# First two batches transposed from fp32 and loaded a second time, a new order of the weight loads, and paired squares, in a fused attention and feed-forward kernel

## The chip, the cores and the metric

The kernel runs on one core of one Trainium2 chip. The metric is device microseconds of that core, the median over the executions of a call; below, "before" in a comparison always means executions of the kernel before in the same call, on the same chip. The span of a profile is some 1.8 us shorter than the time of the same execution.

## The reference

Two small attentions between `x` (8 batches, 8 heads, 512 tokens, 64 wide) and `state` (32 rows per head), then a feed-forward layer with squared ReLU over all 4608 resulting rows. Cut to what matters:

```python
scores = scale * x @ state.T          # x reads the state
a      = softmax(scores);   xread = a @ state
scores2 = scale * state @ x.T         # the state reads x
a2     = softmax(scores2);  sread = a2 @ x          # needs x itself
x = concat([xread, sread], axis=2) -> (4608, 512)
h = x @ w_in                          # 512 x 2048
g = s * relu(h)**2 + b
out = g @ w_out                       # 2048 x 512
```

## The kernel before

A small scheduler written in the kernel takes a list of operations with estimated durations, needs, buffers and order constants, and fixes the order of instructions on each engine. PE (TensorE) forms `M = state @ w_in` for each batch and then `h = a.T @ M`; ScalarE (ACT) does the exponentials, logarithms and most ReLUs; VectorE (DVE) squares, makes pair sums and scales the output. The heavy output products start with `o <- wo,g`.

The parts that the change touches. The weights and the x of batches 2 and up are loaded by one software queue issued from GpSimd (POOL), in a fixed order; the x of batches 0 and 1 comes in fp32 by other queues, is cast to fp16 (`xn`), and transposed by PE:

```python
SEQ = "wi0 wi2 wo1 wi1 wo0 wi3 wo2 wo3 x2 x3"      # wi: w_in chunk, wo: w_out part
...
add(AC(0.5) if n < 3 else (DV(0.35), AC(0.5)), ..., cast_x(b, i),       # 8 casts fp32 -> fp16
    [("xf", b, i)], [("x", b, i)], [("u", f"xf{n // 2}"), ("xn", f"x{b}")])
...
def xT_mm(b, i):                                   # 8 transposes, fp16
    ps = A[b][f"xTps{i}"] = att_ps([P, 4, 2, P], FP16, ...)
    mm(ps[:, hh, k, :], xn[b][:, head_of(i, hh), ...], ident16, is_transpose=True)
```

`V` is the product `a2 @ x`, named "slot reads" in the title of the change. It needs `xn`, and `aT`: the exponentials `E`, transposed by a DMA that SyncE (SP) issues, four such DMAs for the first two batches:

```python
def aT_dma(b, g):
    nc.sync.dma_start_transpose(a["aT"][:, g], a["E"][g])
...
add(PEt(0.22), kV, V_mm(b), [("aT", b, 0), ("aT", b, 1)], [("V", b)],
    [V_b, ("aT", f"aT{b}"), xn_b], tiled=True)
...
def square(name, f):                               # one block of 512
    ENG[e].tensor_mul(g_of(name, f), g_of(name, f), g_of(name, f))
```

Near 33 us PE also forms the "bias sums" (`wsum_ps`), which need all four parts of `w_out`.

The softmax here doesn't subtract the row's maximum and nothing guards it: scores larger than these inputs give would overflow.

## Time and profile before

| | kernel before |
|---|---|
| time, median of 3 (range) | 210.81 us (210.65 to 210.86) |
| span of the profiled execution (211.43 us, 0.6 above the median) | 209.6 us |
| PE / DVE / ACT busy | 97% / 84% / 65% |
| first `h` matmul / first output matmul | 15.24 / 24.07 us |
| the four `aT` transpositions landed | 36.0 to 38.7 us |

Its busy line, its chain of work, the windows of the start and the timeline rows there are in the prediction. Needed for comparison is the page: the row of the software queue (packets, MB, share of the 16 DMA engines' span), what was read from memory, and the group of the squares (busy us, mean ns, idle before).

```profile
q0 software_dynamic: 12896, 14.68, 37.4%
...
HBM read 17.33 MB, written 8.91 MB: 125 GB/s over the span
...
L813 DVE TENSOR_TENSOR g<-g 128x512 f16<-128x512 f16 x128 | 52.7, 423 | 5.1 <-ACT g L807 3.3
```

```profile
40.00:45.00 5.00, 5.00 (x98) 2.22 (x96) 4.96 (x9) 1.67 (x3) 3.73 (x6) 1.00 0.67 183
```

### The profile page before, as it was taken

What the parts mean: (1) busy time and instruction counts of PE and PEld (TensorE: products, weight loads), DVE (VectorE), ACT (ScalarE), POOL (GpSimd) and SP (SyncE); (2) the same over time, 40 slices, a digit from 0 to 9 for tenths busy, and PEclk for the clock granted to TensorE, in tenths of its full rate; (3) what the DMA queues carried; (4) which work ended last, traced back from release to release, by engine and by line L of the source; (5) the groups of instructions that cost most, each with busy time, mean ns of one, the idle gap of its engine ahead of it and who ended that gap; (6) DMA issues with size and microseconds to landing.
All of it is one profiled execution on the core that took longest, in us unless ns stands there. A gap on an engine that the chain in (4) does not pass through costs nothing.

```text
span 209.6 us, 4981 instructions
## 1 busy us (share of the span) xinstructions
PE 202.7 (97%) x1962; PEld 131.3 (63%) x1962; DVE 176.0 (84%) x406; ACT 135.7 (65%) x302; POOL 41.1 (20%) x65
## 2 busy tenths in 40 slices
PE   7998999999999999999999999999999999999993
PEld 2532344434865766677667766776667777788882
DVE  2569999998779898899989998998899989867762
ACT  3899899658578857775776658675767545236300
POOL 0850000150250225022501331121012001200000
PEclk9999999999999999999999999999999999999999
DMA  6999999589898763933298339421302111310132
GB/s 194 299 191 204 214 205 159 124 183 119 193 159 116 119 141 77 160 103 112 69 122 160 105 70 157 107 81 49 100 9 100 50 53 50 100 59 2 47 133 75
DMA packets 42344, 25.00 MB, mean 119 GB/s; under 512 B 26448, under 2 KB 40528, under 8 KB 42320
## 3 DMA queue, kind: packets, MB, share of 16 engines
q0 software_dynamic: 12896, 14.68, 37.4%
q1 hardware_dynamic: 29136, 9.84, 24.9%
q8 instruction: 15, 0.25, 0.5%
q10 hardware_dynamic: 288, 0.16, 0.4%
q14 instruction: 9, 0.07, 0.1%
HBM read 17.33 MB, written 8.91 MB: 125 GB/s over the span
## 4 chain that ended last, share of the span: by engine, by line
PE 87%; DMA 9%; POOL 2%; SPq 0%; DVE 0%; issue 0%
PE o L214 49%; PE h L214 24%; DMA wo<-in_moe_w_out_dram 7%; PE Mps L214 4%; PE h_sr L214 3%; PE osr L214 3%; DMA xf<-in_x_dram 2%; PE V L214 1%; PE D L214 1%; POOL wi L362 1%; PE T L214 1%; PE wsum_ps L214 0%; SPq L256 0%; POOL wo L372 0%; DVE c_sr L1052 0%; PE bias_ps L214 0%
## 5 line engine op out<-in xcount | busy, mean ns | idle before, releaser
L807 ACT ACTIVATE g<-h 128x512 f16<-128x512 f32 x125 | 72.8, 599 | 39.4 <-PE h L214 38.7
L214 PE MATMUL h<-a,M 128*128 128x512 f16 x256 | 74.0, 379 | 0.7 <-ACT g L807 0.7
L813 DVE TENSOR_TENSOR g<-g 128x512 f16<-128x512 f16 x128 | 52.7, 423 | 5.1 <-ACT g L807 3.3
L214 PEld LDWEIGHTS <-pd 128*128 128x128 f16 x448 | 42.6, 98 | 20.7 <-issue 4.2
L214 PEld LDWEIGHTS <-g 128*128 128x128 f16 x400 | 38.7, 98 | 20.1 <-issue 1.6
L214 PE MATMUL o<-u,pd 128*128 128x256 f16 x336 | 48.8, 273 | 0.0
L214 PE MATMUL o<-wo,g 128*128 128x256 f16 (+1 forms) x288 | 45.8, 296 | 0.3 <-DMA wo<-in_moe_w_out_dram 0.3
L1064 POOL DMA_DIRECT2D out_dram<-c x24 | 16.4, 682 | 100.8 <-DVE c L1052 97.4
L214 PEld LDWEIGHTS <-M 128*128 128x128 f16 x256 | 24.5, 98 | 12.8 <-issue 3.4
L306 ACT CAST M<-Mps 128x512 f16<-128x512 f32 x41 | 22.8, 592 | 4.7 <-PE Mps L214 4.7
L1052 DVE SCALAR_TENSOR_TENSOR c<-o,sb_cols,bias_bc 128x512 f32<-128x512 f32 x28 | 21.0, 750 | 5.6 <-PE o L214 5.1
L829 DVE TENSOR_TENSOR pd<-g 128x1024 f16<-128x1024 f16 x28 | 19.2, 687 | 0.4
L1052 DVE SCALAR_TENSOR_TENSOR c<-o,sb_cols,c 128x512 f32<-128x512 f32 x21 | 15.7, 750 | 4.5 <-PE o L214 4.1
L214 PE MATMUL o<-u,g 128*128 128x256 f16 x112 | 17.2, 273 | 0.0
L308 DVE CAST M<-Mps 128x512 f16<-128x512 f32 x23 | 15.1, 683 | 0.5 <-PE Mps L214 0.4
L214 PE MATMUL o<-wo,pd 128*128 128x256 f16 x112 | 15.4, 273 | 0.0
L385 POOL DMA_DIRECT2D xn<-in_x_dram x18 | 13.9, 824 | 0.0
L550 ACT ACTIVATE E<-T 128x256 f16<-128x256 f32 x32 | 11.4, 386 | 2.5 <-PE T L214 2.5
L840 DVE TENSOR_TENSOR pd<-g,pd 128x512 f16<-128x512 f16 x28 | 11.7, 419 | 0.3
L838 DVE TENSOR_TENSOR pd<-g,pd 128x512 f16<-128x512 f16 x28 | 11.7, 416 | 0.1
L573 ACT ACTIVATE D<-D 128x512 f32<-128x512 f32 x16 | 9.3, 588 | 1.9 <-PE D L214 1.9
L580 ACT ACTIVATE R<-D 128x512 f16<-128x512 f32 x16 | 9.4, 597 | 0.4
(80 smaller groups left out, 158.5 us busy)
## 6 DMA issues: line engine op xcount, KB each, us to landing
out_dram<-c POOLq DMA_DIRECT2D x24, 256.0 KB, 2.6
xf<-in_x_dram SPq DMA_DIRECT2D x8, 256.0 KB, 5.0
wi<-in_moe_w_in_dram POOLq DMA_DIRECT2D x4, 512.0 KB, 9.9
wo<-in_moe_w_out_dram POOLq DMA_DIRECT2D x4, 512.0 KB, 16.2
xn<-in_x_dram POOLq DMA_DIRECT2D x16, 128.0 KB, 4.2
xn<-in_x_dram POOLq DMA_DIRECT2D x2, 512.0 KB, 15.1
out_dram<-osb POOLq DMA_DIRECT2D x4, 256.0 KB, 2.9
out_dram<-c SPq DMA_DIRECT2D x4, 256.0 KB, 2.5
```

Of the source, the lines that this page charges most:

```text
L214: return nc.tensor.matmul(out, lhsT, rhs, start=start, stop=stop, tile_position=tp, is_transpose=is_transpose, skip_group_check=True,)
L306: nc.scalar.copy(dst, src)
L308: ENG[e].tensor_copy(dst, src)
L385: nc.gpsimd.dma_start(out=xn[b][:, h0:h1].rearrange("p h c d -> p h (c d)"), in_=x[b, h0:h1].rearrange("h (q c) d -> q h (c d)", q=P),)
L550: nc.scalar.activation(a["E"][g][:, 256 * m : 256 * m + 256], a["T"][m][:, g, :], AF.Exp, scale=scale, **kw)
L807: nc.scalar.activation(g_of(name, f), OSB["h", name, f], AF.Relu)
L813: ENG[e].tensor_mul(g_of(name, f), g_of(name, f), g_of(name, f))
L829: nc.vector.tensor_tensor(pd[:, :, 0:2], g4[:, :, 1:2, :].to_broadcast((P, 2, 2, t)), g4[:, :, 0:4:3, :], ALU.subtract,)
L838: nc.vector.tensor_tensor(pd[:, :, 2], g4[:, :, 3], pd[:, :, 0], ALU.subtract)
L840: nc.vector.tensor_tensor(pd[:, :, 3], g4[:, :, 2], pd[:, :, 2], ALU.subtract)
L1052: nc.vector.scalar_tensor_tensor(t, src, s_bc, add, ALU.mult, ALU.add)
L1064: ENG[e].dma_start(dst[:, rows:SCH:2, hD * h : hD * h + hD], SN[b, name])
```

## The change

The intent is to start PE's real work earlier. The cast of `x` leaves the head of the kernel: PE transposes the fp32 tiles directly. As `V` still needs `x` in fp16, the x of batches 0 and 1 is loaded a second time, casting on the way, behind the weights ("late for the slot reads"). Three chunks of `w_in` now come ahead of most of `w_out`. Squares go two blocks at a time, the logarithm of the softmax sums goes to SBUF (freeing a PSUM slot), and all order constants of the scheduler are retuned. The core of the diff:

```diff
-    for n in range(8):                       # the eight casts of x
-        add(AC(0.5) if n < 3 else (DV(0.35), AC(0.5)), ..., cast_x(b, i), ...)
+    add(DV(0.15), -31, lambda e: nc.vector.tensor_copy(ident32, ident16), ...)
...
-    SEQ = "wi0 wi2 wo1 wi1 wo0 wi3 wo2 wo3 x2 x3"
+    SEQ = "wi0 wi1 wi2 wo0 wo1 wi3 wo2 x2 wo3 x0 x1 x3"
...
-            ps = A[b][f"xTps{i}"] = att_ps([P, 4, 2, P], FP16, ...)
-                    mm(ps[:, hh, k, :], xn[b][...], ident16, is_transpose=True)
+            ps = A[b][f"xTps{p}"] = att_ps([P, 2, 2, P], FP32, ...)
+                    mm(ps[:, hh, k, :], xf_part(b, p)[:, hh, P * k : P * k + P], ident32, is_transpose=True)
...
-            nc.scalar.activation(A[b][f"D{g}"], A[b][f"D{g}"], AF.Ln)
+            A[b][f"L{g}"] = opool.tile([P, S], FP32, ..., tag="osb")
+            nc.scalar.activation(A[b][f"L{g}"], A[b][f"D{g}"], AF.Ln)
...
-            PEt(0.22), kV, V_mm(b), [("aT", b, 0), ("aT", b, 1)], [("V", b)],
+            PEt(0.22), kV, V_mm(b), [("aT", b, 0), ("aT", b, 1)] + ([("x", b, i) for i in range(4)] if b < 2 else []), [("V", b)],
...
-            ENG[e].tensor_mul(g_of(name, f), g_of(name, f), g_of(name, f))
+            g = G[name, f // 4][:, f % 4 : f % 4 + 2, :]
+            ENG[e].tensor_mul(g, g, g)
```

Cut: the retuned constants, the scheduler's small additions, other PSUM slots for the first scores and the warm-ups, and the bias that ACT may now do.

## The prediction

> **What bounds the kernel now.** I read the page first: its busy line and its chain of work that ended last.
>
> ```profile
> PE 202.7 (97%) x1962; PEld 131.3 (63%) x1962; DVE 176.0 (84%) x406; ACT 135.7 (65%) x302; POOL 41.1 (20%) x65
> ...
> PE 87%; DMA 9%; POOL 2%; SPq 0%; DVE 0%; issue 0%
> PE o L214 49%; PE h L214 24%; DMA wo<-in_moe_w_out_dram 7%; PE Mps L214 4%; PE h_sr L214 3%; PE osr L214 3%; DMA xf<-in_x_dram 2%; PE V L214 1%; PE D L214 1%; POOL wi L362 1%; PE T L214 1%; PE wsum_ps L214 0%; SPq L256 0%; POOL wo L372 0%; DVE c_sr L1052 0%; PE bias_ps L214 0%
> ```
>
> TensorE (PE) is the bound. The only part of the chain that is not PE is at the start: a load of x (2%), the issue of weight loads, and a wait for w_out (7%). The windows by stage say when. Columns: stretch, its length, then busy us of each engine.
>
> ```profile
> core 0: us, PE busy (x) PEld busy (x) DVE busy (x) ACT busy (x) POOL busy (x), PEclk, DMA share, GB/s
> 0.00:5.00 5.00, 3.81 (x9) 1.16 (x9) 1.14 (x10) 1.90 (x2) 0.20 (x4) 1.00 0.62 185
> 5.00:10.00 5.00, 4.52 (x52) 2.56 (x51) 2.60 (x8) 3.74 (x8) 3.75 (x6) 1.00 1.11 312
> 10.00:15.00 5.00, 4.51 (x55) 1.91 (x53) 3.11 (x7) 4.90 (x13) 3.52 (x5) 1.00 1.21 190
> 15.00:20.00 5.00, 4.30 (x31) 1.48 (x30) 4.57 (x11) 4.77 (x10) 0.24 (x1) 1.00 1.24 204
> 20.00:25.00 5.00, 4.52 (x33) 1.58 (x32) 4.63 (x12) 4.81 (x10) 0.00 (x0) 1.00 1.23 215
> 25.00:30.00 5.00, 5.00 (x38) 2.03 (x37) 4.95 (x16) 4.30 (x10) 0.28 (x1) 1.00 1.24 207
> ...
> 109.93:131.69 21.76, 21.76 (x229) 14.91 (x227) 19.93 (x44) 15.48 (x33) 5.59 (x8) 1.00 0.74 119
> ```
>
> From 25 us on PE is busy in every window; one batch takes 21.77 us and PE works all of it, with VectorE (DVE) at 92% beside it. Before 25 us PE is idle or runs warm-up matmuls, while ScalarE (ACT) is at 95 to 98% and the DMA engines are saturated. So whatever the change does for DVE or ACT after 25 us is worth nothing directly, and only what starts PE's real work earlier, or later makes it wait, moves the end. The timeline of the start shows the first matmul on h, the first output matmul, and what that one waited for; the POOL rows date the landings of the second, seventh and eighth weight.
>
> ```profile
> 13.22 0.41 PE L214 MATMUL Mps<-wi,stT 64*32 64x512 f16 x8
> ...
> 15.24 1.02 PE L214 MATMUL h<-a,M 128*128 128x512 f16 x4
> ...
> 18.58 0.24 POOL L429 CAST stf<-wo 128x2 f32<-128x2 f16 x1 [5.05 <-DMA wo<-in_moe_w_out_dram]
> ...
> 24.07 1.02 PE L214 MATMUL o<-wo,g 128*128 128x512 f16 x4 [0.35 <-DMA wo<-in_moe_w_out_dram]
> ...
> 29.08 0.28 POOL L415 CAST sb_in<-wo 128x2 f32<-128x2 f16 x1 [10.27 <-DMA wo<-in_moe_w_out_dram]
> ...
> 31.67 0.47 POOL L426 CAST stf<-wo 128x2 f32<-128x2 f16 x1 [2.31 <-DMA wo<-in_moe_w_out_dram]
> ```
>
> Landings, issue plus "to landing" in the views of the load lines: w_in chunk 0 at 12.2, the eight weights in queue order 12.2, 14.8, 18.5, 21.0, 24.0, 26.5, 29.0, 31.6, then x of batch 2 (issued 12.6, 22.5 to landing) at 35.1. One weight per 2.8 us, in queue order.
>
> **What the Trainium skill says.** "DMA: Bandwidth & Descriptors", section "SWDGE vs HWDGE vs iDMA": one software queue is allocated, and each DMA engine round-robins between that and the hardware queues. The trace agrees: landings come in issue order, and x of batch 2, beside the transposes issued from 30.8 on, took 3.5 us after its predecessor instead of 2.5. "VectorE: DVE Perf Modes", "Mode 2×_1P": two results per cycle for 16-bit data, one for fp32 or PSUM. Agrees: the fp16 square of 128x512 takes 423 ns and the fp16 subtraction of 128x1024 takes 687, while a 512-wide cast from fp32 PSUM takes 683. "ScalarE: Activation LUTs": ScalarE writes PSUM faster than SBUF. Hardly here: the logarithm that stays in PSUM takes 588 ns, the exponential that goes to SBUF 597. "TensorEngine Tiling (Array Packing)": switching the tiling mode drains PE. Agrees: four h matmuls take 0.86 us start to start, 0.96 where a tiled group follows.
>
> **The change part by part.** Durations are those of the page; but two relus in a row take 1.09 us of ACT and five squares 1.85 us of DVE in the timeline, so the pitch is 0.5 on ACT, and 0.36 (fp16) or 0.6 (from PSUM) on DVE.
>
> 1. *No cast of x.* Six ACT casts (3.7 us) and two DVE casts (0.9) go. The copies after the transposes become eight of 512 fp32 elements: two on ACT, six on DVE (6 x 0.69 = 4.1 us, against 3.2 for all copies before). Net about 3 us off ACT, 1.5 us onto DVE, all before 13 us. The chain to the first exponential loses a cast (0.62): transposes after the 9 warm-ups at 5.1, copy by 6.3, second by 7.1, scores at 7.6, first exponential at 8.0 (before: 8.71). Second pair: 8.75 against 9.78. ACT then has no xn cast between, so the last reciprocal of batch 0 ends at 11.8 rather than 13.18. fp32 transposes may cost PE two to four times the 55 ns of fp16; no trace shows it yet. PE has room: there were 24 warm-ups.
> 2. *But w_in chunk 0 lands at 12.2 in both.* The first product M then runs at 12.3 instead of 13.22, its casts end near 13.4 (DVE has the fourth copy of batch 1 just before), the scores of batch 1 come first in PE's order, and the first h starts at 14.2: 1.0 us earlier, not the 1.4 that ACT alone would give.
> 3. *Loads.* First landings stay 12.2 and 14.8; w_in chunk 2 comes third (near 17.5), w_out part 0 fourth, near 20.9 instead of 24.0. The program's order puts 8 h tiles ahead of the first output group (before: 12), so it is due when it lands. Walking ACT in steps of 0.5 from 15.1 (h0, two logarithms, R, h2, h3, R, h4, h5, an M cast, h6, h7) gives h7 on PE at 19.9 and one M group behind it at 20.5 to 20.8. First output group: 21.0.
> 4. *From there to the bias sums.* Nine groups of 0.86 and one M pair of 0.66 to the first group with w_out part 2, waiting 0.3 for w_in chunk 3 (26.5): 29.7. Then five groups, one transposition (0.22) and a mode switch (0.1): the bias sums are due at 34.4. By then PE has done two h tiles (0.86) and two output groups (1.73) more than before at its bias sums (32.82), so the equal point of the old kernel is 35.4. **Gain: 1.0 us.**
> 5. *What is loaded late.* x of batch 2 now stands ahead of w_out part 3, so the two exchange landings: part 3 comes at 34 to 35.1. The bias sums need it: 0 to 0.7 us of waiting, 0.2 expected. Then x of batches 0 and 1 (1 MB each, read from HBM) follow for V. At 2.6 to 3.5 us each beside the transposes, and up to 5.7 where transposes are dense (x of batch 3 took 7.7 from issue), the second lands at 41 to 46. V stands in PE's fixed order about 9.7 us behind the bias sums: 44.1 to 44.8. Expected wait 0.3.
> 6. *Pairs of squares.* 64 of about 0.69 for 128 of 0.423: 54 - 44 = 10 us less DVE. It takes DVE from 92 to about 88% of a batch, off the path.
> 7. *Logarithm to SBUF, bias on ACT.* Same durations; a PSUM slot comes free sooner. Nothing on the path.
> 8. *Steady state and end.* The built order has the same matmuls and the same 54 mode switches after the first h; the last group is the same. Zero, if no buffer or relu makes PE wait.
>
> Sum: -1.0 + 0.2 + 0.3 = -0.5 us. The table of order constants was retuned throughout, which my walk cannot value after 45 us; I allow 0.6 more for that and for a start that is better than walked. Predicted 210.81 - 1.1 = 209.7.
>
> **The rivals.** *A, the reload stalls PE.* V waits for the second x; if the queue gets only half of the engines (as x of batch 3 did), it lands at 47, PE waits 2 to 3 us, and the time is 211.5 to 213. For: saturated DMA up to 33 us and eight transposes behind. Against: the DMA share falls to 0.7 to 0.8 after 35. *B, the start gains in full.* DVE and ACT keep up, part 3 and x arrive in time, and the first output group at 21.0 carries nearly all: up to 2.5 us, 208.3. Against: ACT at 95% and four fewer h tiles done by then. *C, the steady state loosens.* New orders bunch h tiles; ACT needs 0.5 per relu plus casts, PE would wait a few tenths in each of six batches: 211 to 212. Against: ACT is at 70% per batch. *D, nothing.* Old loads bounded the start, new ones do: 210.8.
>
> **Range and chances.** What the start could give is limited: PE lacks about 2.3 us of work between its first h and 24 us, plus 1 to 1.4 ahead of that. So faster by over 2% (4.2 us) would need more than there is: 0.03. Slower by 2% needs rival A with over 4 us: 0.04. Range 208.2 (B) to 211.4 (mild A or C).
>
> **What the new profile would show.** Right: first h near 14.2, first output group at 20.8 to 21.3, waits of PE on wo and xn under 1 us together, batches still 21.8 us, DVE squares near 44 us. Wrong: PE waiting more than 1.5 us for xn or wo, the first output group after 22, a batch that differs from 21.77 by over 0.2, or PE idle after 50 us.

## More of the kernel before

```profile
DMA to landing us min/median/max: 2.5/3.9/5.2
```

PE has no gap there, the DMA engines are two thirds busy, and the slowest of the four `aT` lands 5.2 us after its issue.

## The result and the profile after

The kernel after took **210.42 us** (median of four, 210.38 to 210.91), the kernel before 210.84 (210.65 to 211.2). The ratio is 0.9984, with a 95% interval of 0.9964 to 1.0004: not clearly different at all. A ratio is the mean time of one kernel's fast runs over that of the other's of the same rounds, so it is not quite the ratio of the medians quoted. A gain of 1.1 us had been forecast; 0.4 came.

The page after: busy line, software queue, memory read, the chain of work by engine and by line, and the group of the squares.

```profile
PE 201.8 (97%) x1957; PEld 132.4 (63%) x1957; DVE 168.1 (81%) x334; ACT 133.0 (64%) x297; POOL 42.6 (20%) x67
...
q0 software_dynamic: 14976, 15.73, 40.6%
...
HBM read 19.43 MB, written 8.91 MB: 136 GB/s over the span
...
PE 77%; DMA 17%; POOL 3%; DVE 1%; SPq 0%; issue 0%
PE o L214 44%; PE h L214 20%; DMA wo<-in_moe_w_out_dram 10%; DMA aT<-E 4%; PE h_sr L214 3%; PE osr L214 3%; PE Mps L214 3%; DMA xf<-in_x_dram 2%; POOL wi L342 1%; PE D L214 1%; PE V L214 1%; POOL wo L352 1%; PE T L214 1%; SPq L256 0%; POOL xn L365 0%
...
L791 DVE TENSOR_TENSOR g<-g 128x1024 f16<-128x1024 f16 x64 | 43.5, 686 | 4.7 <-ACT g L784 4.1
```

DVE lost 7.9 us of work, 9.2 of it in the squares, and PE is still the bound. The 2.1 MB more that are read are the second load of x. New in the chain is `DMA aT<-E` at 4%, which was not in the chain of before.

The timeline of PE's start: the first fp32 transposes, the first `M` product, the first `h`, the first output group.

```profile
4.70 0.60 PE L214 MATMUL xTps<-ident,xf 128*128 128x128 f32 x4
...
12.12 0.96 PE L214 MATMUL Mps<-wi,stT 64*32 64x512 f16 x16
...
13.67 1.03 PE L214 MATMUL h<-a,M 128*128 128x512 f16 x4
...
20.40 1.02 PE L214 MATMUL o<-wo,g 128*128 128x512 f16 x4 [0.22 <-DMA wo<-in_moe_w_out_dram]
```

So `h` starts at 13.67 and not at 15.24, and the output products at 20.40 and not at 24.07. Nothing is wrong with the start. The windows after say where to look next:

```profile
40.00:45.00 5.00, 4.03 (x82) 1.60 (x82) 4.13 (x8) 4.49 (x9) 2.11 (x5) 1.00 1.26 222
...
109.93:131.69 21.76, 21.76 (x229) 14.91 (x227) 19.07 (x37) 15.13 (x35) 5.61 (x8) 1.00 0.62 114
```

In the steady state (last row) PE works all the time, as before, with DVE at 88% of the stretch and not 92%. But between 40 and 45 us, where PE had worked 5.00 of 5.00 us, it now works 4.03, and the DMA share is 1.26 against 0.67. The timeline there shows why:

```profile
43.45 0.55 PE L214 MATMUL V<-xn,aT 128*32 128x64 f16 x48
44.98 0.30 PE L214 MATMUL V<-xn,aT 128*32 128x64 f16 x16 [0.97 <-DMA aT<-E]
45.21 0.61 PE L214 MATMUL h<-a,M 128*128 128x512 f16 x2
```

PE reaches `V` at 43.45, does 48 of its 64 matmuls, and stops for the last `aT`. The second x, which the prediction had in mind, had landed at 42.33. The tile view of `aT`, again from 28 to 42 us, agrees (who waited for it, us and times; then issue to landing):

```profile
  PE V L214: 1.0, 1
...
DMA to landing us min/median/max: 7.4/9.1/9.5
```

**A ledger.** To see gains and losses along the way I added up, for each trace, the matmul work in PE's order (columns of every matmul that is not a warm-up or a transpose), and compared the times at which two kernels reach the same amount. "Lead" is by how much a kernel is ahead of the second profile of the kernel before (e1_before below, 211.05 us). The first profile of before lags that one by 0.38 us from the bias sums on, so a start counted against it looks that much better.

| profiled execution | time us | last `aT` issued, landed | PE reached `V` | stop at `V` | lead at 42 us | lead just after `V` | lead late (near 198 us) |
|---|---|---|---|---|---|---|---|
| after | 210.38 | 35.72, 44.93 | 43.45 | 1.13 | 1.54 | 0.37 | 0.67 |
| after (e2_after) | 210.07 | 35.57, 44.64 | 43.62 | 0.66 | 1.37 | 0.67 | 0.97 |
| after (e3_after) | 209.87 | 35.56, 44.39 | 43.52 | 0.52 | 1.48 | 0.91 | 1.22 |
| squares single (e2_single) | 209.77 | 35.77, 43.72 | 43.98 | 0 | 1.01 | 0.97 | 1.27 |
| no reload (e2_poolfix) | 209.73 | 35.81, 38.98 | 43.93 | 0 | 1.06 | 1.02 | 1.31 |
| `V` later (e1_vlate) | 209.23 | 35.80, 45.26 | 47.47 | 0 | 1.64 | 1.69 | 1.84 |
| `V` later (e3_vlate) | 209.69 | 35.63, 43.87 | 47.97 | 0 | 1.14 | 1.18 | 1.34 |

The stop is the time from the first matmul of `V` to the first one behind it, less the 0.63 us that `V` takes undisturbed (in e2_single and e2_poolfix). Of a start lead of 1.4 to 1.5 us the kernel after gives back 0.6 to 1.2 at `V`. The column at 42 us is the softest, as the kernels have different matmuls behind them there: a recount gives 1.32, 1.16, 1.26, 0.85, 0.85, 1.42 and 0.92 at 38 us, where they have done nearly the same. The drop at `V` does not hang on it; it is the stop, read from the timelines. Between 76 us and the end all these kernels gain another 0.3 us or a little more. Most of it is in the matmuls' start times: in both profiles of the kernel before, an `h` behind ten output products starts 74 ns late once a batch (at 94, 116, 138 and 159 us, each time released by a ReLU on ACT); in the traces of after, e2_single, e2_poolfix and `V` later it does not. Such a gap is too short for the timeline to mark.

### The profile page after: what moved, and what is told of

The parts are those of the page before. It is cut to its first block, busy times and chain, and to the rows that moved or that the text cites. A ratio compares the mean times of both kernels' runs of the same rounds, so it can differ in the third digit from the quotient of the medians.

```text
span 208.6 us, 4904 instructions
## 1 busy us (share of the span) xinstructions
PE 201.8 (97%) x1957; PEld 132.4 (63%) x1957; DVE 168.1 (81%) x334; ACT 133.0 (64%) x297; POOL 42.6 (20%) x67
## 4 chain that ended last, share of the span: by engine, by line
PE 77%; DMA 17%; POOL 3%; DVE 1%; SPq 0%; issue 0%
PE o L214 44%; PE h L214 20%; DMA wo<-in_moe_w_out_dram 10%; DMA aT<-E 4%; PE h_sr L214 3%; PE osr L214 3%; PE Mps L214 3%; DMA xf<-in_x_dram 2%; POOL wi L342 1%; PE D L214 1%; PE V L214 1%; POOL wo L352 1%; PE T L214 1%; SPq L256 0%; POOL xn L365 0%
## 5 line engine op out<-in xcount | busy, mean ns | idle before, releaser
L214 PE MATMUL o<-u,pd 128*128 128x256 f16 x336 | 49.8, 273 | 0.0
L791 DVE TENSOR_TENSOR g<-g 128x1024 f16<-128x1024 f16 x64 | 43.5, 686 | 4.7 <-ACT g L784 4.1
L305 ACT CAST M<-Mps 128x512 f16<-128x512 f32 x37 | 20.6, 603 | 8.2 <-PE Mps L214 8.0
L307 DVE CAST M<-Mps 128x512 f16<-128x512 f32 x27 | 17.8, 685 | 0.5
L365 POOL DMA_DIRECT2D xn<-in_x_dram x20 | 15.7, 826 | 5.4 <-DMA wi<-in_moe_w_in_dram 4.9
L214 PE MATMUL o<-u,g 128*128 128x256 f16 x112 | 16.6, 273 | 0.0
L818 DVE TENSOR_TENSOR pd<-g,pd 128x512 f16<-128x512 f16 x28 | 11.8, 422 | 0.5
L529 ACT ACTIVATE E<-T 128x256 f16<-128x256 f32 x24 | 8.9, 384 | 5.1 <-PE T L214 5.0
L560 ACT ACTIVATE R<-L 128x512 f16<-128x512 f32 x16 | 10.1, 630 | 0.5
L553 ACT ACTIVATE L<-D 128x512 f32<-128x512 f32 x16 | 9.4, 595 | 1.2 <-PE D L214 1.0
```

Of the source, the lines that this page charges most:

```text
L214: return nc.tensor.matmul(out, lhsT, rhs, start=start, stop=stop, tile_position=tp, is_transpose=is_transpose, skip_group_check=True,)
L305: nc.scalar.copy(dst, src)
L307: ENG[e].tensor_copy(dst, src)
L365: nc.gpsimd.dma_start(out=xn[b][:, h0:h1].rearrange("p h c d -> p h (c d)"), in_=x[b, h0:h1].rearrange("h (q c) d -> q h (c d)", q=P),)
L560: nc.scalar.activation(A[b][f"R{g}"], A[b][f"L{g}"], AF.Exp, scale=-1.0)
L791: ENG[e].tensor_mul(g, g, g)
```

## The experiments

The theory after the first result: **the reload of x holds up the transpositions of E, and PE, now earlier than before, stops for them at `V`.** The rivals: the missing part went elsewhere (the fp32 transposes, the pairs of squares, a looser steady state), or the start never gave what was forecast and other parts did. All 15 runs gave correct results.

### The same two kernels again: e1_after, e1_before, e2_after, e3_after

No edit. e1_before is one look at the kernel before.

> The changed kernel once more, to fix its ratio. Main theory: the start is worth 1.2 to 1.3 us up to the bias sums, the stop before V (1.1 us, for the transposed aT) takes most of it back, the rest comes after 50 us; ratio 0.998, median 0.3 to 0.6 us under before, and again a stop of 0.8 to 1.3 us at V with aT landing 7 us or more after its issue. Rival: the first profile's stop at V was an accident of that run; then it is missing here.

> The kernel before, for a second profile only: the first one belongs to a run of 211.43 us, 0.6 above its median, and its x landed 0.4 us later than in the changed kernel's profile though the issues are the same. Expected: span near 209.0, x of batch 0 landed near 6.5 for the fourth part and the first w_in chunk near 11.8, so that 0.4 us of the difference between the two profiles belongs to the run and not to the change.

> The changed kernel a third time, because the two ratios so far differ (0.998 and 0.9925) and the profile of the second was of a freak execution. Theory: the ratio depends on how late aT lands, that is on the DMA engines' luck of a run; expected 0.992 to 0.998, and in the profile a stop of PE before V whose length goes with the landing of the last aT (about 1.1 us where that lands at 45). Rival: the two chips differ throughout, and the stop at V is the same in all.

> The changed kernel again, beside the kernel with V later on the same chip. Theory: 1.0 to 1.5 us under the kernel before, with a stop before V of 0.5 to 1.1 us in the profile. Rival (the first ratio, 0.998, was the usual one): 0.4 us under before.

| call | after, median us | before, median us | ratio (95%) |
|---|---|---|---|
| on record | 210.42 | 210.84 | 0.9984 (0.9964 to 1.0004) |
| e1 | 209.83 | 211.15 | 0.9925 (0.9887 to 0.9962) |
| e2 | 209.93 | 211.09 | 0.9944 (0.9930 to 0.9958) |
| e3 | 210.28 | 211.18 | 0.9958 (0.9928 to 0.9988) |

So the difference of the medians was 0.4, 1.3, 1.2 and 0.9 us: the first call was the smallest of four, and the ratio of 0.998 expected of e1_after did not come again. In three later calls the kernel after is clear of noise, by about what was forecast. The profiled execution of e1_after took 1168.21 us; its PE was busy all the time, and its matmuls followed each other some six times as slowly. No other execution was like it; nothing in the profile explains it, and it is left out.

The two good traces of this kernel show the same stop, with another size. The timeline of e3_after:

```profile
43.52 0.56 PE L214 MATMUL V<-xn,aT 128*32 128x64 f16 x48
44.44 0.30 PE L214 MATMUL V<-xn,aT 128*32 128x64 f16 x16 [0.36 <-DMA aT<-E]
```

And the waits of e2_after:

```profile
PE V L214 <- DMA aT<-E: 0.5, 1, 0.5
```

In the table above, the last `aT` lands at 44.93, 44.64 and 44.39, steps of 0.29 and 0.25; the executions end in steps of 0.31 and 0.20. In these three traces (no more than three points) the end follows that landing almost one to one, although PE reached `V` within 0.17 us each time. The kernel before splits `V` in two and does not stop at either half (timeline of e1_before):

```profile
42.50 0.42 PE L214 MATMUL V<-xn,aT 128*32 128x64 f16 x32
...
43.81 0.42 PE L214 MATMUL V<-xn,aT 128*32 128x64 f16 x32
```

### `V` later: e1_vlate and e3_vlate

```diff
-            [V_b, ("aT", f"aT{b}"), xn_b], tiled=True,
+            [V_b, ("aT", f"aT{b}"), xn_b], tiled=True, after=47.0 if b < 2 else 0.0,
```

The loads and the transpositions of E stay, and PE's order is unchanged up to `V`; PE does other work first. Behind it the scheduler also moved a few instructions of the other engines.

> The changed kernel with V of batches 0 and 1 placed later in PE's order (after the first four groups of w_out part 2, some 4 us later), every earlier PE instruction unchanged. Main theory: nothing waits for aT or x any more, and the time falls by about 1.0 us against the changed kernel: 209.3 to 209.6, ratio near 0.993. Rival (V only showed a wait that would otherwise stand elsewhere): within 0.2 us of the changed kernel.

> V later, second time. Theory: 0.3 to 0.8 us under the changed kernel of this job, as much as its stop before V. Rival (the wait at V hides time that is lost elsewhere anyway, or the stop is there only with the profiler): equal within 0.15 us.

Measured: 209.51 us against 211.15 (0.9912, 0.9879 to 0.9945), and 209.73 against 211.18 (0.9932, 0.9912 to 0.9952). The timeline of e3_vlate shows `V` in one piece behind an output group:

```profile
47.00 1.04 PE L214 MATMUL o<-wo,g 128*128 128x512 f16 x4
47.97 0.70 PE L214 MATMUL V<-xn,aT 128*32 128x64 f16 x64
```

The stop is gone and the lead is kept (1.64 to 1.69, 1.14 to 1.18). Beside the kernel after of the same call the median is 0.32 and 0.55 us lower. The intervals of the two overlap in each call, so by the times alone that step is likely and not settled (if the fast executions are shuffled at random within each call, a gap of the means this large comes up in about 2 of 100 cases); the traces show the stop's removal plainly. Against the kernel before, both calls are clear: **this version has a lower median than both kernels in both calls**, about 1.5 us under before. Its 12 executions lie between 209.23 and 210.13, the 17 fast ones of the kernel after in e1 to e3 between 209.43 and 210.93.

### `V` earlier: e3_vearly

```diff
-V0=39.2, V1=31.3,
+V0=20.0, V1=20.0,
...
-V_mm(b), [("aT", b, 0), ("aT", b, 1)] + ([("x", b, i) for i in range(4)] if b < 2 else []), [("V", b)],
-            [V_b, ("aT", f"aT{b}"), xn_b], tiled=True,
+V_mm(b), [("aT", b, 0), ("aT", b, 1)] if b >= 2 else [], [("V", b)],
+            [V_b, ("aT", f"aT{b}"), xn_b], tiled=True, after=38.3 if b < 2 else 0.0,
```

The scheduler is told that `V` of the first two batches needs nothing, so that it places it early; the real waits on the data stay.

> V 5.8 us earlier in PE's order than in the changed kernel (behind the bias sums' second pair of h groups), the PE order up to there unchanged. Theory: the landing of the last aT, at 44 to 45 us, is the barrier, so PE stops some 6 to 7 us at V and the time is 5 to 6 us over the changed kernel: 215 to 216. Rival (aT comes late in the changed kernel only because of what runs meanwhile): the stop is under 3 us.

Measured: 217.53 us against 211.18 (1.0315, 1.0277 to 1.0354), 7.3 slower than after in the same call and not 5 to 6. PE's timeline:

```profile
39.38 0.30 PE L214 MATMUL V<-xn,aT 128*32 128x64 f16 x16 [0.35 <-DMA xn<-in_x_dram]
43.22 0.71 PE L214 MATMUL V<-xn,aT 128*32 128x64 f16 x32 [3.54 <-DMA aT<-E]
44.88 0.40 PE L214 MATMUL V<-xn,aT 128*32 128x64 f16 x16 [0.94 <-DMA aT<-E]
45.21 1.89 PE L214 MATMUL o<-wo,g 128*128 128x512 f16 x4
```

Reached at 38.87, `V` still ends at 45.2: the landing of `aT` (here 44.83) is the barrier, wherever `V` stands. x itself costs 0.35, `aT` 4.5. The last row is a second cost: four matmuls take 1.89 us after this pause instead of 1.03, 420 ns each start to start instead of 216. The Trainium skill, "TensorE: Matmul & The Clock Gate", "What's actually happening", says that after an idle window of about 3.4 us the array runs at half its clock; the 3.54 us of idle time and the doubled pitch agree, and the granted clock from 45.00 to 47.50 us is 0.50. The stop at `V` is 5.7 us (38.87 to 45.21, less 0.63), and the six slow matmuls behind it cost 1.2; the ledger's lead falls by the sum of the two.

### No reload, other casts, same order: e2_poolfix, and e2_vpool with `V` later as well

```diff
+            if b < 2:
+                for i in range(4):
+                    nc.gpsimd.tensor_copy(xf_heads(xn[b], i).rearrange(...), xf_part(b, i))
+                return
             nc.gpsimd.dma_start(out=xn[b][...], in_=x[b, ...])
```

GpSimd casts the fp32 tiles that are there in place of the two loads. The order of instructions on PE, ACT, DVE and SP is that of the kernel after. e2_vpool adds the line of e1_vlate.

> The changed kernel with the second load of x of batches 0 and 1 replaced by casts of the fp32 tiles on GpSimd, at the same place of its program, so that every instruction of PE, ACT, DVE and the DMA issues of SP stands exactly as in the changed kernel. Theory (the reload's traffic makes aT late): aT lands by 40 us, PE does not stop at V, and the time is that of the changed kernel less its stop: 209.2 to 209.5. Rival (GpSimd casts or something else cost as much): the stop is there, or the lead is already smaller at 30 us.

> V later and the casts on GpSimd together, the order of the kernel with V later. Theory: each removes the same stop, so the two together are worth no more than either: 209.2 to 209.6, within 0.2 us of the kernel with V later. Rival: the reload also slows something after V (the outputs and x of batch 3 behind it), then 0.3 us or more under both.

Measured: e2_poolfix 209.73 against 211.09 (0.9945, 0.9928 to 0.9963), e2_vpool 209.75 (0.9937, 0.9924 to 0.9949), with e2_after at 209.93 (0.9944). The tile view of `aT` from 28 to 42 us and PE's timeline of e2_poolfix:

```profile
DMA to landing us min/median/max: 2.8/3.9/5.7
```

```profile
43.93 0.70 PE L214 MATMUL V<-xn,aT 128*32 128x64 f16 x64
```

Without the reload the slowest of the four transpositions needs 5.7 us and not 9.5, the last lands at 38.98, and `V` does not stop. So the reload is the cause of the late `aT`, which is the theory's middle link. The other traces agree: in the nine with the reload the last `aT` lands between 43.72 and 45.26, in the seven without it (both of before among them) between 38.54 and 40.03. One row of each trace shows where it is felt on SP, the issue of the last `aT` in the kernel after and in e2_poolfix (start, us):

```profile
35.72 4.45 SPq L608 DMA_TRANSPOSE aT<-E  x1
```

```profile
35.81 1.20 SPq L612 DMA_TRANSPOSE aT<-E  x1
```

With the reload in the queues the issue itself takes 4.45 us instead of 1.20. Yet the time is that of after, within 0.2 us, and not the 209.2 to 209.5 that the theory asked for. In e2_poolfix the profiled start was simply later: its lead was 1.15 us at 27 us, against 1.40 to 1.57 in the profiled executions of after. In e2_vpool the start was the best of all (1.74), but w_out part 3 landed at 34.14 instead of 33.6 to 33.7, and the bias came late for PE, as its waits show:

```profile
PE bias_ps L214 <- DVE wsum L909: 0.3, 1, 0.3
```

The lead falls from 1.50 to 1.00 there. This is a second barrier: in e2_single, below, part 3 landed at 34.22 with the reload in place, and the lead falls by 0.28 at the same point. Why part 3 is late in some executions is not shown. In three of the four profiled kernels with the new load order and no reload (e2_poolfix, e2_vpool, e1_pool) it landed 5.8 to 6.2 us behind part 2, with the reload 5.2 to 5.5; so taking the reload away may have a cost of its own there, which no run tests. Taking the reload away thus removes the stop and gives no clear gain in time; in the profiled executions the start and this wait take up the difference, and for the others it is open.

### The same idea, replanned: e1_pool

```diff
-    SEQ = "wi0 wi1 wi2 wo0 wo1 wi3 wo2 x2 wo3 x0 x1 x3"
+    SEQ = "wi0 wi1 wi2 wo0 wo1 wi3 wo2 x2 wo3 x3"
+    add(("POOL", 0.85), -25 + 0.1 * n, cast_x(b, i), ...)      # eight casts
```

> The changed kernel without the second load of x: the fp32 tiles that are there already are cast to fp16 on GpSimd (8 casts of about 0.83 us between 13 and 20 us), V where the planner puts it. Main theory: the transposes of aT land again near 38 to 39 us as in the kernel before, V does not wait, and the time falls by about 1 us against the changed kernel. Rival: aT is late for another reason (its own later issue), V still waits about 1 us. Second rival: the casts on GpSimd slow DVE or hold the buffers of the weight sums, and the gain of the start shrinks.

Measured: 211.75 against 211.15 (1.0015, 0.9976 to 1.0053). A miss, and an inconclusive one: the scheduler, given other operations, put all engines in another order, and its constants are tuned to a given list. The theory's link held in its trace (the last `aT` landed at 40.03, and `V` did not stop), but w_out part 3 came at 34.64, and PE lost some 0.8 us around the bias sums. It led to e2_poolfix, where the order is kept.

### Squares one block at a time again: e2_single

```diff
-            g = G[name, f // 4][:, f % 4 : f % 4 + 2, :]
-            ENG[e].tensor_mul(g, g, g)
+            for k in range(2):
+                ENG[e].tensor_mul(g_of(name, f + k), g_of(name, f + k), g_of(name, f + k))
```

> The changed kernel with each pair of squares split again in two of 512 columns, at the same place: order of all engines as before. DVE gets some 10 us more busy. Theory (DVE is off the path): within 0.3 us of the changed kernel of this job. Rival (DVE at 81% sets buffers free late in the start): 0.5 us or more slower.

Measured: 209.51 against 211.09 (0.9926, 0.9913 to 0.9938), no slower than e2_after (0.9944, 0.9930 to 0.9958), rather 0.4 us faster, for a reason that is not shown; the intervals overlap. The group of the squares:

```profile
L791 DVE TENSOR_TENSOR g<-g 128x512 f16<-128x512 f16 x128 | 47.8, 418 | 0.8 <-ACT g L784 0.8
```

DVE works 171.8 us instead of 168.1, and the time does not rise: **the pairs of squares are worth nothing here**. In the profiled execution the last `aT` landed at 43.72, before PE came to it, so there was no stop.

### The load order: e3_seqold, e4_seqnew and e4_vlwo3

e3_seqold is the kernel after with the order of weights of before; e4_seqnew is the kernel before with the new order of weights; e4_vlwo3 is `V` later, with w_out part 3 ahead of x of batch 2 again. All three are replanned by the scheduler.

```diff
 # e3_seqold, from after
-    SEQ = "wi0 wi1 wi2 wo0 wo1 wi3 wo2 x2 wo3 x0 x1 x3"
+    SEQ = "wi0 wi2 wo1 wi1 wo0 wi3 wo2 x2 wo3 x0 x1 x3"
 # e4_seqnew, from before
-    SEQ = "wi0 wi2 wo1 wi1 wo0 wi3 wo2 wo3 x2 x3"
+    SEQ = "wi0 wi1 wi2 wo0 wo1 wi3 wo2 wo3 x2 x3"
 # e4_vlwo3, from e1_vlate
+    SEQ = "wi0 wi1 wi2 wo0 wo1 wi3 wo2 wo3 x2 x0 x1 x3"
```

> The changed kernel with the weights loaded in the order of the kernel before (w_in 0, w_in 2, w_out 1, w_in 1, w_out 0, w_in 3, w_out 2, x2, w_out 3, x0, x1), replanned. Theory (most of the start's lead is w_out part 0 landing as the fourth rather than the fifth): the first output group goes from about 20.5 back to 24, and the lead over the kernel before at the bias sums from 1.4 to under 0.6 us; time 210.3 to 211. Rival (the lead comes from the shorter chain through ACT): still 1 us under before.

> The kernel before with the new order of the weight loads alone (w_in 0, 1, 2, w_out 0, 1, w_in 3, w_out 2, 3, x2, x3), replanned. Theory (the load order alone carries the start's lead): the first output group comes near 21 instead of 24 and the time falls by 1 us or more. Rival (the lead needs the shorter chain of the fp32 transposes as well): within 0.5 us of before, or slower for the untuned order.

> V later, and w_out part 3 loaded ahead of x of batch 2, replanned. Theory (after the start PE waits for nothing but V and mode switches, and the bias sums did not wait for part 3): within 0.3 us of the kernel with V later, 209.3 to 209.9. Rival (part 3 held the bias sums): 0.5 us faster than that.

Measured: e3_seqold 212.74 against 211.18 (1.0079, 1.0054 to 1.0104), beyond the 210.3 to 211 expected. With the fp32 transposes kept, the first output group comes late again, in its timeline:

```profile
23.81 1.02 PE L214 MATMUL o<-wo,g 128*128 128x512 f16 x4
```

e4_seqnew: 211.39 against 211.23 (0.9998, 0.9981 to 1.0016). The output group comes at 21.75, but the first `h` is late, and ACT's cast of x is among what PE waits for (timeline and waits):

```profile
16.09 1.02 PE L214 MATMUL h<-a,M 128*128 128x512 f16 x4
```

```profile
PEld L214 <- ACT xn L306: 1.3, 2, 0.8
```

So the new order alone gave nothing here, and the rest without it lost. Neither is the worth of a part: both kernels were replanned with constants tuned to another order. A caution: in the profiled execution of e4_seqnew x landed about 1 us later than usual, so its 16.09 is partly that; the medians don't depend on it. e4_vlwo3: 209.86 against 211.23 (0.9935, 0.9920 to 0.9950), the same as `V` later without it. The exchange of x of batch 2 and w_out part 3 costs nothing.

### The casts of x back again: e4_cast

```diff
-            for p in range(4):               # fp32 transposes, reload in SEQ
+            add(AC(0.5) if n < 3 else (DV(0.35), AC(0.5)), ..., cast_x(b, i), ...)
+            for i in range(2):               # fp16 transposes as before, no reload
```

> The changed kernel with x cast to fp16 on ACT and DVE ahead of the transposes again, as before the change, and no second load; new load order, pairs of squares and constants kept, replanned. Theory (the chain through ACT counts beside the loads): the first h starts 1 us or more later than in the changed kernel, aT lands by 39, V does not stop, and the time is 0.5 to 2 us over the changed kernel. Rival (only the load order counts): equal or faster, since nothing is reloaded.

Measured: 214.59 against 211.23 (1.0174, 1.0147 to 1.0201), but confounded: the scheduler put all products `M` of the first chunk in a row, and the first `h` came at 18.63, at half the clock (0.50 granted from 18 to 20 us, with no idle time of PE above 0.63 us before it, so a pause like that of e3_vearly is not the only way there):

```profile
18.63 1.93 PE L214 MATMUL h<-a,M 128*128 128x512 f16 x4
```

That the casts cost something is consistent with this; how much can't be read from it.

## Why the prediction was right or wrong

**Forecast 209.7, a gain of 1.1 us; measured in the first call 0.4, in three later calls 1.3, 1.2 and 0.9.** The place of the gain was right, and so was rival A's place of the loss. The size of the loss was wrong. In the profiled execution of the first call the ledger has 1.5 at the start, 1.2 lost at `V` and 0.3 gained later, 0.67 in sum against the second profile of before.

- **Bound.** Right. PE works all of 109.93 to 131.69 in both kernels by its busy time, and the squares did not move the end (e2_single gives them back at no cost). "PE works all of it" hid one small thing, the 74 ns a batch for which PE waited on ACT in the kernel before.
- **Steps 1 to 4, the start.** Right, a little low. The first `M` product came at 12.12 (12.3 forecast), 0.3 behind the landing of w_in chunk 0; `h` at 13.67 (14.2); the first output group at 20.40 (21.0), waiting 0.22 for w_out part 0; the bias sums at 33.71 (34.4). Against the equal point 35.4 of the first profile that is a gain of 1.7 us, against that of the second (35.0) 1.3; step 4 had 1.0. The ledger has 1.2 to 1.3 against the second profile at 38 us and 1.4 to 1.5 at 42. The fp32 transposes cost twice fp16 (below), within the assumed two to four times.
- **Step 5, first half, w_out part 3.** Allowed 0.2. It landed at 33.64, no wait of PE for it is in the profile, and e4_vlwo3 gains nothing by undoing it. In two other executions (e2_single, e2_vpool) it came at 34.1 to 34.2, and 0.3 to 0.5 went at the bias, so the term was of a fair size and does not always fall due.
- **Step 5, second half: the step that failed.** "The second lands at 41 to 46" was right (42.33), and `V` was only about 1 us earlier than "44.1 to 44.8" (43.45). But "Expected wait 0.3" looked at x alone. `V` has two inputs, and the transpositions of `E`, which run beside the reload (DMA share 1.26 from 40 to 45 us against 0.67), were delayed more: the last landed at 44.4 to 44.9 in place of 38.7. The wait was 0.52 to 1.13 us. Taking away the reload (e2_poolfix) brings the transpositions back to 38.98 and removes the stop; moving `V` back (e1_vlate, e3_vlate) removes it with the reload in place; moving it forward (e3_vearly) makes it larger, and it ends at the same landing. The prediction had the number that mattered, x beside the transposes, and applied it in one direction only; and it took the load of the DMA engines at that time ("0.7 to 0.8 after 35") from the kernel before, without the reload.
- **The allowance of 0.6.** It had no working. By the ledger the start gave 0.2 to 0.5 of it, and about 0.3 came after 75 us, most of it from the 74 ns a batch that PE no longer waits. The term was about right in sum, and that is luck in part: no working led to it.
- **Steps 6 to 8.** Right, but for these 74 ns a batch. Squares 43.5 us (44); the logarithm and its exponential changed by 1 and 6%.
- **Rivals.** A was right in kind and far too large: 0.5 to 1.1 us of wait, not 2 to 3, for `aT` and not for x. B's end did not come, but the start gain is real. C and D are out. Of the signs of being wrong that it listed none came: they watched waits for xn and wo, and none watched `aT`.
- **Its sums and readings.** Small slips, none of which moves the result: the first POOL row dates the third weight, not the second; step 4 adds up to 34.3, not 34.4; in step 1 the two DVE casts that go (0.9) were not taken off, so DVE gains 0.6 us and not 1.5; two loads of 2.6 to 5.7 us from 34 to 35.1 end between 39 and 46.5, not from 41 on. And that whatever lies in PSUM goes at the single rate does not fit the trace of before: a copy of 512 fp16 columns out of PSUM takes 421 ns there, about what the square in SBUF takes (423).

**Why 0.4 in the first call and about 1.1 later** is only partly settled. Shown: the stop differs from execution to execution with the landing of one transposition, 1.13 in the profiled one of the first call against 0.66 and 0.52, and the end moves with it. Not shown: that the three other executions of the first call had a stop as long, as only profiled executions have traces; and the kernel before was itself 0.3 us faster in that call than in the others, which the change has nothing to do with. The calls e1 to e3 ran on chips 3, 13 and 13; which chip ran the first is not on record, so a difference between chips is not ruled out either.

## What to carry to other kernels

When a load is added or moved beside other transfers, ask not only whether it arrives in time, but whose transfer it delays, and list every input of the first product that stands behind: here x came in time and a transposition that nobody had touched did not. An earlier start is kept only as far as the next barrier whose time it does not move, so after winning a microsecond at the head, look for the first fixed landing and put other work ahead of it; one constant removed the stop here, and probably the 0.3 to 0.5 us that it cost. And a piece tuned together with its scheduler's order should be tested with the order frozen, as e1_pool and e4_cast show by failing to tell anything.

## What the Trainium skill lacked or had wrong

- "DMA: Bandwidth & Descriptors", "SWDGE vs HWDGE vs iDMA", says that a DMA engine round-robins between the software and hardware queues, and not what that does to a transposition beside software loads. Here the slowest of four took 9.5 us from issue to landing with two 1 MB loads in the software queue, 5.7 without (e2_poolfix), and SP was held 4.45 us instead of 1.20 at the last issue.
- "TensorE: Matmul & The Clock Gate", Part 4, gives a time of a 128x128 bf16 transpose (about 275 to 390 ns) but none for fp32. In these traces one fp32 transpose takes about 270 ns (the row of four, 0.60 us, less three steps), close to the page's bf16 figure, and one fp16 transpose 220; but fp32 ones follow each other every 109 ns, fp16 ones every 56. It is this pitch that a kernel pays in a row of them, and Part 4 has it for neither type.
- "ScalarE: Activation LUTs" ranks PSUM as the faster destination of ScalarE. The logarithm went from 588 ns to 595 when its destination became SBUF, about 1%; reading it back from SBUF instead of PSUM raised the exponential from 597 to 630 ns, 6%. The source mattered more than the destination.
- No page has the scatter of the first landings: w_in chunk 0, first in the queue in every kernel here, landed between 11.8 and 13.3 us. The start depends on such landings: in the ten profiles that keep PE's order of after up to the bias sums or close to it, the lead at 27 us fell from 1.7 to 0.4 us as w_out part 0 landed from 20.2 to 21.5. Nor anything like the single execution of 1168 us.
